# Attention, two mixture layers, one core: GpSimd's elementwise work moved to ScalarE and VectorE

## The chip, the cores and the metric

The kernel runs on one core of a Trainium2 chip. A core has TensorE (matrix products; the profile tells its products, PE, from its weight loads, PEld), VectorE (DVE), ScalarE (ACT), GpSimd (POOL) and SyncE (SP), which issues most DMAs here. Each engine works through its own queue in order and waits on semaphores for the others. The metric is the device time of one execution in microseconds; smaller is better.

## The reference

Three stages follow each other, all float32 (q, k and the last layer's weights are drawn with the spreads the reference sets):

```python
# attention: q, k, v of shape (4, 8, 576, 64), blocks of 64
scores = (q @ k.T) / 8;  scores = where(block_i >= block_j, scores, -1e9)
attn = exp(scores - max) ;  attn = attn / (sum(attn) + 1e-9);  x = attn @ v   # -> (2304, 512)
# first layer: w1, w2, w3 of (512, 768), w_out of (768, 512), held as int64 images of float64 values
h = maximum(maximum(x @ w1, x @ w2), x @ w3);  x = h @ w_out                   # -> (2304, 512)
# last layer: 8 experts of (512, 1024) and (1024, 512)
active = x @ w_skip > 0;  e = argmax(x @ w_gate);  p = softmax(x @ w_gate)[e]
out = x;  out[active] += p * (relu(x @ w1[e]) @ w2[e])
```

## The kernel before

The 2304 tokens are cut into nine chunks of 256. Attention works in 80 *units*: one pair of heads and up to 128 queries (64 in "packed" units, which put both heads into one set of 128 partitions), with 64 to 576 keys. A unit goes through four functions, and three units are under way at a time: unit k in `s_scores`, k-1 in `s_norm` and `s_trans`, k-2 in `s_pv`.

- `s_scores`: TensorE forms `sc` from `q` and `k` (L231) and adds the mask by a small product (L238). VectorE reduces to the negated maximum `nm` (L244, L249, L252, with L247 or L253 where there are two parts), ScalarE takes the exponential with `nm` as bias and sums it (L258). `q` has been multiplied by 0.125 ahead by GpSimd in `prep` (L209). Where the keys don't fill 128 columns, GpSimd clears 64 more (L260).
- `s_norm`: `r` is the sum plus 1e-9 (L270 on VectorE, L273 on GpSimd for chunks 0 to 2, else on VectorE), its reciprocal is taken (L274), and `p` is multiplied by it: on GpSimd for chunks 0 to 3 (L278), on VectorE for the others (L280).
- `s_trans`: TensorE transposes `p` (L293), ScalarE or VectorE copies it out of PSUM (L295, L297).
- `s_pv`: the product with `v` (L312); ScalarE writes the result's high part (L314), VectorE the low part `x` (L315).

The first layer's products run on pairs of a high part (rounded to the product's format) and a low part (what is left), three products for one. `wprep` makes the weights' pairs, 24 tiles of 128x512: a DMA on SP's queue into one of three raw buffers (L148, or L155 for `w_out`), then `decode`: the absolute value on ScalarE (L137), four VectorE operations (L138 to L141), the second half of which reads the raw buffer. ScalarE then writes the high part (L158) and GpSimd the low part `lo` (L159). Tiles 18 to 23 (`w_out`) also go through TensorE to make the routing weights `wp`.

`m_h` does the first layer for one chunk and one of six slices of the hidden width: three groups of twelve products (L327) into one of two PSUM buffers, ScalarE copies the first (`ha`, L331), VectorE takes the maximum (`hm`, L334), ScalarE writes the high part `h_h` (L338), GpSimd the low part `h_l` (L339). `m_logits` (L348) reads `h_h` and `h_l` for the routing, `m_y` (L364) multiplies by `w_out`. Routing (`r_gate`, `r_rank`) and the last layer (`Moe2`, with its own splits into high and low parts on all three engines, L633 and L637) follow.

The program is written as a loop over units; a credit hands out steps of the first layer between them, and `wprep` is called four times per unit until tile 18. The order that each engine gets in the end is made by a planner, which sorts the instructions by its own estimates of when each is ready and gives attention a higher priority than weights and first layer. The last steps of the first layer and the last layer keep the order in which they are written. The `x` tiles have two buffers, so attention for chunk c+2 can't write `x` before chunk c's `m_h` has read it.

Of the kernel before, what the change touches and what calls it, by code (L numbers as in the profile page):

```python
# [12 lines left out]
AF = mybir.ActivationFunctionType  # L13
ALU = mybir.AluOpType
# [7 lines left out]
P = 128  # L22
# [3 lines left out]
ND = DM // P  # L26
# [64 lines left out]
def _moe1_phase(tc, nc, const, small, g):  # L91
# [10 lines left out]
    with ExitStack() as st_y:  # L102
# [25 lines left out]
        raw_t = [apool.tile([P, 4 * P, 2], I32, name=f"raw{i}") for i in range(3)]  # L128
# [13 lines left out]
            return uf  # L142

        def wprep(k):
            raw, dec = raw_t[k % 3], dec_t[k % 6]
            if k < 18:
                f, i = divmod(k, 3)
                nc.sync.dma_start(  # L148
                    out=raw.rearrange("p (c f) t -> p c (f t)", c=ND),
                    in_=ws[i][:, 2 * f * P:2 * (f + 1) * P].rearrange("(c p) f -> p c f", p=P))  # L150
                c = decode(raw, dec).rearrange("p (c f) -> p c f", c=ND)
                hi, lo = w_piece(f, i, 0), w_piece(f, i, 1)
            else:
                f = k - 18
                nc.sync.dma_start(out=raw.rearrange("p f t -> p (f t)"), in_=w_out[f * P:(f + 1) * P, :])  # L155
                c = decode(raw, dec)
                hi, lo = wo[0][:, f, :], wo[1][:, f, :]
            nc.scalar.copy(hi, c)  # L158
            (nc.vector if (0 and k % 0 == 0) else nc.gpsimd).tensor_tensor(lo, c, hi, op=ALU.subtract)  # L159
            if k >= 18:  # L160
                ps = ps_m.tile([P, ND, P], F32, tag="mo", name="pswt")
                for d in range(ND):
                    nc.tensor.transpose(ps[:, d, :], c[:, d * P:(d + 1) * P], ident)
                wt = tmp.tile([P, ND, P], F32, tag="y", name="wt")
                nc.scalar.copy(wt, ps)
                ps = ps_m.tile([P, NG], F32, tag="mo", name="psw")
                for d in range(ND):
                    nc.tensor.matmul(ps, wt[:, d, :], wr_sb[:, d, :], start=(d == 0), stop=(d == ND - 1))
                nc.vector.tensor_copy(wp[:, f, 0:NG], ps)
                nc.vector.tensor_tensor(wp[:, f, NG:2 * NG], ps, wp[:, f, 0:NG], op=ALU.subtract)  # L170
# [24 lines left out]
        def load_v(i):  # L195
            if i >= len(groups):
# [5 lines left out]
            nc.sync.dma_start(  # L202
                out=gd["v"][:, 0:nkt, :],
                in_=v[b, 0:nkt * P, hp * P:(hp + 1) * P].rearrange("(t p) d -> p t d", p=P))

        def prep(i):
            if i < len(groups):
                q = gdat[i]["q"][:, 0:groups[i][3] - groups[i][2]]
                nc.gpsimd.tensor_scalar(q, q, 0.125, None, op0=ALU.mult)  # L209

        units = []
        for i, (c, b, qlo, qhi, tiles, hp) in enumerate(groups):
# [5 lines left out]
        def s_scores(k):  # L218
            i, c, hp, q0, nq, nk, col, first = units[k]
            gd, u = gdat[i], ud[k]  # L220
            packed = nq == 64
            parts = [(0, nk)] if nk <= 512 else [(0, nk // 2), (nk // 2, nk)]
            sets = 1 if packed else 2
            banks = {}
            for n, (lo, hi) in enumerate(parts):
                if n == 0 or not packed:
                    ps = ps_s.tile([P, 2, 512], F32, tag="sc", name="sc")
                for j in range(2):
                    bank = banks[j, n] = ps[64 * j:64 * j + 64, n] if packed else ps[:, j]
                    rows = slice(64 * j, 64 * j + 64)  # L230
                    nc.tensor.matmul(bank[:, 0:hi - lo], gd["q"][rows, q0:q0 + nq], gd["k"][rows, lo:hi],  # L231
                                     start=True, stop=packed or hi != nk)
                if n == 0:
                    first_ps = ps
                if hi == nk and not packed:
                    for j in range(2):
                        rows = slice(64 * j, 64 * j + 64)
                        nc.tensor.matmul(banks[j, n][:, hi - lo - 64:hi - lo], mask_q[rows], mask_k[rows],  # L238
                                         start=False, stop=True)
            pt = pp.tile([P, 2, 5 * P], F32, tag="p", name="p")  # L240
            nm = sm.tile([P, 2], F32, tag="nm", name="nm")
            w = parts[0][1]
            if packed:
                nc.vector.tensor_reduce(nm[:, 0:len(parts)], first_ps[:, 0:len(parts), 0:w], axis=AX.X, op=ALU.max,  # L244
                                        negate=True)
                if len(parts) == 2:
                    nc.vector.tensor_tensor(nm[:, 0:1], nm[:, 0:1], nm[:, 1:2], op=ALU.min)  # L247
            else:
                nc.vector.tensor_reduce(nm, first_ps[:, :, 0:w], axis=AX.X, op=ALU.max, negate=True)  # L249
                if len(parts) == 2:  # L250
                    nm2 = sm.tile([P, 2], F32, tag="nm2", name="nm2")
                    nc.vector.tensor_reduce(nm2, ps[:, :, 0:w], axis=AX.X, op=ALU.max, negate=True)  # L252
                    nc.vector.tensor_tensor(nm, nm, nm2, op=ALU.min)  # L253
            su = sm.tile([P, 2, 2], F32, tag="su", name="su")
            for j in range(sets):
                for n, (lo, hi) in enumerate(parts):
                    src = first_ps[:, n, 0:hi - lo] if packed else banks[j, n][:, 0:hi - lo]
                    nc.scalar.activation(pt[:, j, lo:hi], src, AF.Exp, bias=nm[:, j:j + 1], accum_out=su[:, n, j:j + 1])  # L258
            if nk % P:
                nc.gpsimd.memset(pt[:, 0:sets, nk:nk + 64], 0.0)  # L260
            u.update(p=pt, su=su, parts=len(parts), sets=sets)

        def s_norm(k):
            i, c, hp, q0, nq, nk, col, first = units[k]
            u = ud[k]
            su, sets = u["su"], u["sets"]
            r = sm.tile([P, 2], F32, tag="r", name="r")
            eng = nc.gpsimd if c < 3 else nc.vector
            if u["parts"] == 2:
                nc.vector.scalar_tensor_tensor(r[:, 0:sets], su[:, 0, 0:sets], 1e-9, su[:, 1, 0:sets],  # L270
                                               op0=ALU.add, op1=ALU.add)
            else:
                eng.tensor_scalar(r[:, 0:sets], su[:, 0, 0:sets], 1e-9, None, op0=ALU.add)  # L273
            nc.vector.reciprocal(r[:, 0:sets], r[:, 0:sets])  # L274
            for j in range(sets):
                pt = u["p"][:, j, 0:nk]
                if c < 4:
                    nc.gpsimd.tensor_tensor(pt, pt, r[:, j:j + 1].to_broadcast([P, nk]), op=ALU.mult)  # L278
                else:
                    nc.vector.tensor_scalar(pt, pt, r[:, j:j + 1], None, op0=ALU.mult)  # L280

# [36 lines left out]
        def m_h(c, f):  # L318
            xh, xl = xt[c]
            h_h, h_l = hid[c // (NCH - 1)]  # L320
            prev = None
            for i in range(3):
                ps = ps_m.tile([P, CH], F32, tag="mo", name="ps_h")
                n = 0
                for d in range(ND):
                    for a, x in ((w_piece(f, i, 0), xh), (w_piece(f, i, 0), xl), (w_piece(f, i, 1), xh)):
                        nc.tensor.matmul(ps, a[:, d, :], x[:, d, :], start=(n == 0), stop=(n == 3 * ND - 1))  # L327
                        n += 1
                if i == 0:
                    prev = tmp.tile([P, CH], F32, tag="hm", name="ha", bufs=4)  # L330
                    nc.scalar.copy(prev, ps)  # L331
                else:
                    nxt = tmp.tile([P, CH], F32, tag="hm", name=f"hm{i}", bufs=4)
                    nc.vector.tensor_tensor(nxt, ps, prev, op=ALU.max)  # L334
                    prev = nxt
                if i < 2:
                    yield
            nc.scalar.copy(h_h[:, f, :], prev)  # L338
            nc.gpsimd.tensor_tensor(h_l[:, f, :], prev, h_h[:, f, :], op=ALU.subtract)  # L339
            yield  # L340

        def m_logits(c, rd):
# [120 lines left out]
            nc.vector.memset(mask_q[r:r + 1, 0:64], 1.0)  # L463
            nc.vector.memset(mask_k[r:r + 1], -float(2 ** 30))
        load(0)
        prep(0)
        nc.sync.dma_start(out=g["cst_sb"], in_=g["cst"])
        load_v(0)
        load(1)
# [33 lines left out]
        for k in range(n_u + 2):  # L503
            if k < n_u:
                i, c, first = units[k][0], units[k][1], units[k][-1]
                if first:
                    load(i + 2)
                    load_v(i + 1)
                with pri(c):
                    s_scores(k)  # L510
                if first:
                    prep(i + 1)
            if 0 <= k - 1 < n_u:
                with pri(units[k - 1][1]):
                    s_norm(k - 1)
# [318 lines left out]
```

## Time and profile before

| | us |
|---|---|
| median of 3 runs (lowest, highest) | 749.91 (748.97, 750.33) |
| profiled execution: its time | 748.17 |
| profiled execution: its span, first to last instruction | 746.4 |
| busy: TensorE products / weight loads | 660.3 (88%) / 539.7 |
| busy: VectorE / ScalarE / GpSimd | 405.6 (54%) / 298.2 (40%) / 315.2 (42%) |

The profile is of one execution, 1.7 us below the median of the timed runs; its own time is 1.8 us above its span. Busy shares are means over the whole span, and stages differ much, so the rows below come from views of single stretches. In a view that groups instructions, a line gives the code line, engine and operation, output and inputs, tile, count, then busy time in us and the mean of one in ns, then idle time ahead of them and what ended it.

### The profile page before, as it was taken

Reading aid. Unit: us, or ns where it says so; the run is one execution under the profiler, and the core shown is the slowest. Engines: PE = TensorE matmul, PEld = TensorE weight load, DVE = VectorE, ACT = ScalarE, POOL = GpSimd, SP = SyncE. Lnnn points to the kernel's source line nnn. Section 1 sums busy time; section 2 is a strip of 40 time slices with the busy share of each in tenths; the row PEclk is TensorE's granted clock in tenths of the full one; section 3 lists DMA queues with packets and bytes.
Section 4 is the critical chain, followed back from the end, with each engine's and each line's share of the span. In section 5 each row is a group of like instructions: output and inputs, shape, how many; then the busy total and the mean of one; then the engine's idle time right before and its main releaser. Section 6 shows DMA issues by size and latency. Waiting matters only on the chain. (4 is left out here: it accounts for less than half of the span.)

```text
span 746.4 us, 13347 instructions
## 1 busy us (share of the span) xinstructions
PE 660.3 (88%) x4854; PEld 539.7 (72%) x4854; DVE 405.6 (54%) x915; ACT 298.2 (40%) x751; POOL 315.2 (42%) x346
## 2 busy tenths in 40 slices
PE   5764789999999999999999999999988938786786
PEld 3432578868978987978888887888978726565665
DVE  4999994344246436346434646534237127477763
ACT  4555554443143325234233434424243125163552
POOL 5986884435231202102113222111039239285775
PEclk9997999999999999999999999999999978898989
DMA  6765433221022212011102112002337659566731
GB/s 178 200 196 170 153 111 84 72 77 38 19 78 70 74 58 78 17 45 55 35 31 71 53 49 65 19 18 76 113 113 252 237 152 339 196 187 218 249 130 31
DMA packets 74520, 82.26 MB, mean 110 GB/s; under 512 B 11284, under 2 KB 51348, under 8 KB 74432
## 3 DMA queue, kind: packets, MB, share of 16 engines
q1 hardware_dynamic: 70768, 75.69, 32.4%
q0 software_dynamic: 2624, 5.45, 2.4%
q8 instruction: 48, 0.79, 0.4%
q14 instruction: 40, 0.33, 0.1%
q10 hardware_dynamic: 1040, 0.01, 0.1%
HBM read 70.44 MB, written 11.96 MB: 110 GB/s over the span
## 5 line engine op out<-in xcount | busy, mean ns | idle before, releaser
L327 PE MATMUL ps_h<-x,w 128*128 128x256 f32 x1944 | 269.1, 291 | 12.0 <-DVE hm L334 6.5
L327 PEld LDWEIGHTS ps_h<-x,w 128*128 128x128 f32 x1944 | 243.6, 193 | 33.7 <-issue 13.9
L258 ACT ACTIVATE p<-sc,nm 128x288 f32<-128x288 f32 (+8 forms) x168 | 84.6, 513 | 39.0 <-PE tp L293 20.2
L209 POOL TENSOR_SCALAR q<-q 128x256 f32<-128x256 f32 (+3 forms) x48 | 37.2, 775 | 127.5 <-DMA q<-in_kqT_dram 107.9
L637 POOL TENSOR_TENSOR lo<-raw,hi 128x1024 fp32r<-128x1024 f32 x30 | 83.0, 2788 | 16.4 <-ACTq L765 15.2
L231 PE MATMUL sc<-k,q 64*128 64x288 f32 (+9 forms) x384 | 78.8, 491 | 10.1 <-POOL q L209 8.8
L293 PE MATMUL tp<-cst_sb,p 128*128 128x128 f32 x432 | 76.6, 295 | 12.0 <-DVE x L315 6.9
L339 POOL TENSOR_TENSOR h_l<-hm,h_h 128x256 fp32r<-128x256 f32 x54 | 42.7, 791 | 98.7 <-ACT h_h L338 98.6
L637 DVE TENSOR_TENSOR lo<-raw,hi 128x1024 fp32r<-128x1024 f32 x30 | 73.5, 2457 | 8.7 <-ACT hi L633 6.4
L312 PE MATMUL pv<-pT,vt 128*64 128x128 f32 (+1 forms) x960 | 68.4, 280 | 7.8 <-ACT pT L295 4.2
L293 PEld LDWEIGHTS tp<-cst_sb,p 128*128 128x128 f32 x432 | 52.1, 148 | 25.5 <-issue 11.3
L295 ACT COPY pT<-tp 128x512 f32<-128x512 f32 (+2 forms) x78 | 40.2, 517 | 70.8 <-PE tp L293 69.8
L633 ACT CAST hi<-raw 128x2048 fp32r<-128x2048 f32 x30 | 56.4, 1902 | 29.1 <-PEq L765 18.5
L312 PEld LDWEIGHTS pv<-pT,vt 128*64 128x64 f32 x960 | 49.8, 141 | 22.8 <-ACT pT L295 6.2
L249 DVE TENSOR_REDUCE nm<-sc 128x2 f32<-128x256 f32 (+7 forms) x64 | 51.6, 810 | 22.0 <-PE sc L238 20.9
L297 DVE COPY pT<-tp 128x512 f32<-128x512 f32 (+2 forms) x58 | 32.0, 551 | 52.3 <-PE tp L293 51.9
L278 POOL TENSOR_TENSOR p<-p,r 128x128 f32<-128x128 f32 (+8 forms) x64 | 52.1, 832 | 19.6 <-DVE r L274 13.0
L334 DVE TENSOR_TENSOR hm<-ps_h,ha 128x256 f32<-128x256 f32 x54 | 22.8, 422 | 54.4 <-PE ps_h L327 48.9
L231 PEld LDWEIGHTS sc<-k,q 64*128 64x128 f32 (+1 forms) x384 | 31.4, 190 | 28.8 <-POOL q L209 10.0
L338 ACT CAST h_h<-hm 128x256 fp32r<-128x256 f32 x54 | 22.0, 407 | 74.1 <-DVE hm L334 73.9
L260 POOL MEMSET p<- 128x128 f32 (+1 forms) x48 | 9.1, 189 | 91.2 <-PE tp L293 83.0
L364 PE MATMUL ps_y<-wo_h,h_h 128*128 128x512 f32 x108 | 43.7, 405 | 0.0
(132 smaller groups left out, 944.0 us busy)
## 6 DMA issues: line engine op xcount, KB each, us to landing
raw<-in_m_w_dram SPq DMA_DIRECT2D x32, 1024.0 KB
raw<-in_w_dram SPq DMA_DIRECT2D x18, 512.0 KB
vt<-in_v_dram SPq DMA_DIRECT2D x16, 320.0 KB
x<-y SPq DMA_DIRECT2D x18, 256.0 KB
out_dram<-y SPq DMA_DIRECT2D x18, 256.0 KB
raw<-in_w_out_dram SPq DMA_DIRECT2D x6, 512.0 KB
vt<-in_v_dram SPq DMA_DIRECT2D x8, 256.0 KB
k<-in_kqT_dram SPq DMA_DIRECT2D x32, 64.0 KB
```

Source lines behind the costliest of these rows:

```text
L231: nc.tensor.matmul(bank[:, 0:hi - lo], gd["q"][rows, q0:q0 + nq], gd["k"][rows, lo:hi], start=True, stop=packed or hi != nk)
L249: nc.vector.tensor_reduce(nm, first_ps[:, :, 0:w], axis=AX.X, op=ALU.max, negate=True)
L258: nc.scalar.activation(pt[:, j, lo:hi], src, AF.Exp, bias=nm[:, j:j + 1], accum_out=su[:, n, j:j + 1])
L278: nc.gpsimd.tensor_tensor(pt, pt, r[:, j:j + 1].to_broadcast([P, nk]), op=ALU.mult)
L293: nc.tensor.transpose(tp[:, n, :], u["p"][:, j, t * P:(t + 1) * P], ident)
L295: nc.scalar.copy(pT[:, t0:t0 + len(part)], tp[:, 0:len(part)])
L312: nc.tensor.matmul(pv[64 * j:64 * j + 64, 0:nq], vt[:, t, 64 * j:64 * j + 64], pT, start=(t == 0), stop=(t == nkt - 1))
L327: nc.tensor.matmul(ps, a[:, d, :], x[:, d, :], start=(n == 0), stop=(n == 3 * ND - 1))
L339: nc.gpsimd.tensor_tensor(h_l[:, f, :], prev, h_h[:, f, :], op=ALU.subtract)
L364: nc.tensor.matmul(ps, a[:, f, hs], x[:, f, :], start=(n == 0), stop=(n == 3 * NF - 1))
L633: self.nc.scalar.copy(self.w(e, s)[0], self.raw_of(4 * e + s))
L637: eng.tensor_tensor(lo[:, r], self.raw_of(4 * e + s)[:, r], hi[:, r], op=ALU.subtract)
```

## The change

`q` is no longer scaled: `prep` is gone, and 0.125 enters the exponential as its scale; the maximum is scaled by VectorE instead. In `s_norm` the `r` addition is always on VectorE; the multiplication of `p` is on ScalarE for chunks 0 to 2 (a copy with a scale per partition), on VectorE from chunk 3 on. The low parts of the weights and of `h` are made on VectorE. In `wprep` the low part of a `w_out` tile now stands behind the transposes. GpSimd keeps the clearing of `p`, constants and DMAs there, and its share of the last layer.

```diff
--- before.py
+++ after.py
@@ -142,25 +142,27 @@
             return uf
 
         def wprep(k):
-            raw, dec = raw_t[k % 3], dec_t[k % 6]
+            raw = raw_t[k % len(raw_t)]
             if k < 18:
                 f, i = divmod(k, 3)
                 nc.sync.dma_start(
                     out=raw.rearrange("p (c f) t -> p c (f t)", c=ND),
                     in_=ws[i][:, 2 * f * P:2 * (f + 1) * P].rearrange("(c p) f -> p c f", p=P))
-                c = decode(raw, dec).rearrange("p (c f) -> p c f", c=ND)
                 hi, lo = w_piece(f, i, 0), w_piece(f, i, 1)
             else:
                 f = k - 18
                 nc.sync.dma_start(out=raw.rearrange("p f t -> p (f t)"), in_=w_out[f * P:(f + 1) * P, :])
-                c = decode(raw, dec)
                 hi, lo = wo[0][:, f, :], wo[1][:, f, :]
+            c = decode(raw, dec_t[k % 6])
+            if k < 18:
+                c = c.rearrange("p (c f) -> p c f", c=ND)
             nc.scalar.copy(hi, c)
-            (nc.vector if (0 and k % 0 == 0) else nc.gpsimd).tensor_tensor(lo, c, hi, op=ALU.subtract)
             if k >= 18:
                 ps = ps_m.tile([P, ND, P], F32, tag="mo", name="pswt")
                 for d in range(ND):
                     nc.tensor.transpose(ps[:, d, :], c[:, d * P:(d + 1) * P], ident)
+            nc.vector.tensor_tensor(lo, c, hi, op=ALU.subtract)
+            if k >= 18:
                 wt = tmp.tile([P, ND, P], F32, tag="y", name="wt")
                 nc.scalar.copy(wt, ps)
                 ps = ps_m.tile([P, NG], F32, tag="mo", name="psw")
@@ -202,11 +204,6 @@
             nc.sync.dma_start(
                 out=gd["v"][:, 0:nkt, :],
                 in_=v[b, 0:nkt * P, hp * P:(hp + 1) * P].rearrange("(t p) d -> p t d", p=P))
-
-        def prep(i):
-            if i < len(groups):
-                q = gdat[i]["q"][:, 0:groups[i][3] - groups[i][2]]
-                nc.gpsimd.tensor_scalar(q, q, 0.125, None, op0=ALU.mult)
 
         units = []
         for i, (c, b, qlo, qhi, tiles, hp) in enumerate(groups):
@@ -251,11 +248,13 @@
                     nm2 = sm.tile([P, 2], F32, tag="nm2", name="nm2")
                     nc.vector.tensor_reduce(nm2, ps[:, :, 0:w], axis=AX.X, op=ALU.max, negate=True)
                     nc.vector.tensor_tensor(nm, nm, nm2, op=ALU.min)
+            nc.vector.tensor_scalar(nm[:, 0:sets], nm[:, 0:sets], 0.125, None, op0=ALU.mult)
             su = sm.tile([P, 2, 2], F32, tag="su", name="su")
             for j in range(sets):
                 for n, (lo, hi) in enumerate(parts):
                     src = first_ps[:, n, 0:hi - lo] if packed else banks[j, n][:, 0:hi - lo]
-                    nc.scalar.activation(pt[:, j, lo:hi], src, AF.Exp, bias=nm[:, j:j + 1], accum_out=su[:, n, j:j + 1])
+                    nc.scalar.activation(pt[:, j, lo:hi], src, AF.Exp, bias=nm[:, j:j + 1], scale=0.125,
+                                         accum_out=su[:, n, j:j + 1])
             if nk % P:
                 nc.gpsimd.memset(pt[:, 0:sets, nk:nk + 64], 0.0)
             u.update(p=pt, su=su, parts=len(parts), sets=sets)
@@ -265,17 +264,16 @@
             u = ud[k]
             su, sets = u["su"], u["sets"]
             r = sm.tile([P, 2], F32, tag="r", name="r")
-            eng = nc.gpsimd if c < 3 else nc.vector
             if u["parts"] == 2:
                 nc.vector.scalar_tensor_tensor(r[:, 0:sets], su[:, 0, 0:sets], 1e-9, su[:, 1, 0:sets],
                                                op0=ALU.add, op1=ALU.add)
             else:
-                eng.tensor_scalar(r[:, 0:sets], su[:, 0, 0:sets], 1e-9, None, op0=ALU.add)
+                nc.vector.tensor_scalar(r[:, 0:sets], su[:, 0, 0:sets], 1e-9, None, op0=ALU.add)
             nc.vector.reciprocal(r[:, 0:sets], r[:, 0:sets])
             for j in range(sets):
                 pt = u["p"][:, j, 0:nk]
-                if c < 4:
-                    nc.gpsimd.tensor_tensor(pt, pt, r[:, j:j + 1].to_broadcast([P, nk]), op=ALU.mult)
+                if c < 3:
+                    nc.scalar.activation(pt, pt, AF.Copy, scale=r[:, j:j + 1])
                 else:
                     nc.vector.tensor_scalar(pt, pt, r[:, j:j + 1], None, op0=ALU.mult)
 
@@ -336,7 +334,7 @@
                 if i < 2:
                     yield
             nc.scalar.copy(h_h[:, f, :], prev)
-            nc.gpsimd.tensor_tensor(h_l[:, f, :], prev, h_h[:, f, :], op=ALU.subtract)
+            nc.vector.tensor_tensor(h_l[:, f, :], prev, h_h[:, f, :], op=ALU.subtract)
             yield
 
         def m_logits(c, rd):
@@ -463,7 +461,6 @@
             nc.vector.memset(mask_q[r:r + 1, 0:64], 1.0)
             nc.vector.memset(mask_k[r:r + 1], -float(2 ** 30))
         load(0)
-        prep(0)
         nc.sync.dma_start(out=g["cst_sb"], in_=g["cst"])
         load_v(0)
         load(1)
@@ -508,8 +505,6 @@
                     load_v(i + 1)
                 with pri(c):
                     s_scores(k)
-                if first:
-                    prep(i + 1)
             if 0 <= k - 1 < n_u:
                 with pri(units[k - 1][1]):
                     s_norm(k - 1)
```

## Rows read from the trace of the kernel before

**Rows 1.** Busy by stage: stretch, length; each engine; granted clock, DMA share, GB/s.

```profile
14.50:112.00 97.50, 67.83 (x404) 46.49 (x403) 95.27 (x148) 55.59 (x143) 79.06 (x76) 0.89 0.58 169
...
130.00:540.00 410.00, 409.56 (x3436) 343.90 (x3431) 189.48 (x608) 148.36 (x484) 94.06 (x166) 1.00 0.18 54
540.00:602.00 62.00, 55.62 (x390) 50.07 (x389) 24.74 (x59) 19.99 (x30) 29.95 (x21) 1.00 0.59 203
602.00:746.40 144.40, 102.22 (x422) 79.78 (x421) 84.86 (x63) 60.61 (x53) 95.60 (x49) 0.86 0.58 188
```

**Rows 2.** TensorE's waits, 130 to 540 us: total us, times, longest.

```profile
PE pv L312 <- DVE pT L297: 0.4, 1, 0.4
```

**Rows 3.** TensorE's waits, 0 to 130 us.

```profile
PE sc L231 <- POOL q L209: 8.8, 3, 6.1
PE tp L293 <- DVE x L315: 6.9, 3, 4.3
```

**Rows 4.** Waits of SP's queue, 0 to 130 us.

```profile
SPq L148 <- DVE dec L141: 16.4, 12, 2.7
```

**Rows 5.** VectorE grouped by line and shape, 14.5 to 112 us.

```profile
L141 DVE SCALAR_TENSOR_TENSOR dec<-raw,dec 128x512 int32<-128x512 int32 x24 | 23.8, 992 | 0.1
L140 DVE SCALAR_TENSOR_TENSOR dec<-raw,dec 128x512 int32<-128x512 int32 x24 | 23.4, 976 | 0.2
L139 DVE TENSOR_SCALAR dec<-dec 128x512 int32<-128x512 int32 x24 | 18.4, 767 | 0.1
L138 DVE TENSOR_SCALAR dec<-dec 128x512 f32<-128x512 f32 x24 | 16.9, 704 | 1.0 <-ACT dec L137 1.0
...
L274 DVE RECIPROCAL r<-r 128x2 f32<-128x2 f32 x13 | 2.0, 158 | 0.4
L334 DVE TENSOR_TENSOR hm<-ps_h,ha 128x256 f32<-128x256 f32 x4 | 1.7, 414 | 1.2 <-PE ps_h L327 1.2
```

**Rows 6.** VectorE in order of time, 46 to 50 us: start, duration, instruction.

```profile
46.27 0.41 DVE L138 TENSOR_SCALAR dec<-dec 128x512 f32<-128x512 f32 x1
46.60 0.68 DVE L140 SCALAR_TENSOR_TENSOR dec<-raw,dec 128x512 int32<-128x512 int32 x1
47.21 0.41 DVE L139 TENSOR_SCALAR dec<-dec 128x512 int32<-128x512 int32 x1
47.54 0.68 DVE L141 SCALAR_TENSOR_TENSOR dec<-raw,dec 128x512 int32<-128x512 int32 x1
...
48.22 1.68 DVE L140 SCALAR_TENSOR_TENSOR dec<-raw,dec 128x512 int32<-128x512 int32 x1
```

**Rows 7.** GpSimd in order of time, 45 to 50 us.

```profile
47.74 1.61 POOL L159 TENSOR_TENSOR w<-dec,w 128x512 fp32r<-128x512 f32 x1
```

**Rows 8.** Single lines over the whole span: count, shortest/median/longest in ns, first and last start.

```profile
L140 DVE SCALAR_TENSOR_TENSOR dec<-raw,dec x24: 673/693/1698, 15.8 to 109.8; 128x512 int32<-128x512 int32 x24
...
L637 DVE TENSOR_TENSOR lo<-raw,hi x30: 1211/1226/8665, 556.4 to 732.0; 128x1024 fp32r<-128x1024 f32 x30
...
L273 DVE TENSOR_SCALAR r<-su x40: 146/169/343, 159.3 to 505.7; 128x2 f32<-128x2 f32 x36, 128x1 f32<-128x1 f32 x4
...
L339 POOL TENSOR_TENSOR h_l<-hm,h_h x54: 722/736/1723, 86.8 to 583.0; 128x256 fp32r<-128x256 f32 x54
```

**Rows 9.** ScalarE grouped by line and shape, 14.5 to 112 us.

```profile
L258 ACT ACTIVATE p<-sc,nm 128x512 f32<-128x512 f32 x8 | 5.5, 692 | 0.0
L258 ACT ACTIVATE p<-sc,nm 128x384 f32<-128x384 f32 x8 | 4.6, 591 | 0.0
...
L258 ACT ACTIVATE p<-sc,nm 128x256 f32<-128x256 f32 x6 | 2.8, 472 | 1.2 <-DVE nm L249 1.2
...
L258 ACT ACTIVATE p<-sc,nm 128x128 f32<-128x128 f32 x4 | 1.5, 381 | 0.0
```

**Rows 10.** GpSimd grouped by line and shape, 0 to 130 us.

```profile
L278 POOL TENSOR_TENSOR p<-p,r 128x512 f32<-128x512 f32 x8 | 10.4, 1320 | 0.3 <-DVE r L274 0.3
```

**Rows 11.** Waits, 530 to 612 us.

```profile
PE ps_l L348 <- POOL h_l L339: 1.1, 2, 0.6
```

## The prediction

> **What bounds the kernel now.** I read the table by stage first [rows 1]. From 130 to 540 us TensorE is busy for 409.56 of 410 us at full granted clock, and the list of its waits for that stretch holds 0.4 us in all [rows 2]. VectorE has 189.48 us of work there, ScalarE 148.36, GpSimd 94.06. So in this long stage TensorE is the bound, and work that moves between the other three changes nothing as long as none of them gets late. From 602 us on runs the last layer, which the change does not touch.
>
> The ramp, 14.5 to 112 us, is the other way round: VectorE is busy for 95.27 of 97.5 us, TensorE only for 67.83, ScalarE for 55.59 [rows 1]. In it the 24 weight tiles are decoded while the first attention units run. TensorE's largest waits up to 130 us are for GpSimd's scaled `q` (8.8 us) and for VectorE's `x` (6.9 us) [rows 3]. SP's queue waits for VectorE too: the next raw weights may only be loaded once a decode has freed their buffer (16.4 us in 12 waits for `w1` to `w3`) [rows 4]. So VectorE sets the length of the ramp, and each us that the ramp loses should come off the end, since TensorE does the same work behind it without a gap.
>
> Why is VectorE full there? Four decode operations a tile make up most of it, with means of 704, 767, 976 and 992 ns [rows 5]. The order in time shows that these are not their own durations: one of each of the four, at 46.27 to 48.2 us, took 0.41, 0.68, 0.41 and 0.68 us, and right after it the same L140 took 1.68 us [rows 6], while GpSimd's `lo` subtraction started at 47.74 and ran for 1.61 us [rows 7]. The shortest L140 is 673 ns, the longest 1698 [rows 8]. VectorE and GpSimd hold each other up, and the change takes GpSimd's elementwise work away.
>
> **The change part by part.**
>
> *Decode without GpSimd.* A tile costs 0.704+0.767+0.976+0.992 = 3.44 us on average [rows 5] against 0.41+0.68+0.41+0.68 = 2.18 us undisturbed [rows 6]. 24 x 1.26 = 30.2 us less on VectorE. From below: nothing, if VectorE's long operations had another cause than GpSimd; from above 30.2, since 2.18 is about the minimum.
>
> *Low parts on VectorE.* 24 new subtractions of 128x512 with two SBUF inputs. The nearest rows are L140, which has the same shape and occupies 0.61 us from its start to the next start (46.60 to 47.21) [rows 6], and the 128x1024 `lo` on VectorE in the last layer, whose minimum and median are 1211 and 1226 ns, half of which is 0.61 [rows 8]. 24 x 0.61 = 14.6 us; at L140's full 0.68 it would be 16.3.
>
> *Small operations.* Each unit gains a multiplication of `nm` by 0.125 and, in chunks 0 to 2, the `r` addition from GpSimd; the ramp holds 14 units (13 reciprocals of two columns [rows 5] and one of one). Each new operation depends on its predecessor; an `r` addition on VectorE takes 0.17 us [rows 8]. 14 x 2 x 0.17 = 4.8 us. Four `h_l` in the ramp at 0.41 us, as the four `hm` of the same shape [rows 5], are 1.7 us.
>
> VectorE's ramp thus loses 30.2 - 14.6 - 4.8 - 1.7 = 9.1 us.
>
> *Scaling on ScalarE.* Two instructions a unit (one in packed units). No row has a copy from SBUF with a scale per partition; the bounds are nothing and the exponential of the same width: 0.692, 0.591, 0.472 and 0.381 us at 512, 384, 256 and 128 columns [rows 9]. With eight of each for chunks 0 and 1 that is at most 17.1 us, and ScalarE would have 55.6 + 17.1 = 72.7 of some 88 us. I take the upper end, and count it at nothing in the sum, because VectorE stays the fuller engine. On the path of one unit it even gains: GpSimd took 1.32 us for 512 columns [rows 10]. The cover is gone if decode's own ScalarE steps (absolute value and the high part's cast) then wait behind it.
>
> The Trainium skill has a rule that speaks against this part: "ScalarE: Activation LUTs", section "Rules for kernel authors", says that multiplications belong on VectorE, not on ScalarE; by its section "What ACT_TABLE_LOAD costs" I estimate 280 + 0.833 x 512 = 707 ns for the wide copy. No run here shows that copy; the exponential of that width, 692 ns, lies close. By that rule alone scaling is best put on VectorE, which would lengthen the full engine; the table by stage decides for ScalarE here.
>
> *`q` no longer scaled.* 0.125 goes into the exponential's scale, which L258 applies without an instruction of its own; the product `q`-`k` then starts when the DMA has landed. TensorE's 8.8 us of waiting for it lie inside the VectorE-bound ramp, so I count nothing, with 8.8 us as the other end.
>
> *Steady stage.* VectorE gets about 43 `h_l` (18 us), 66 `nm` (11 us) and the scaling of chunk 3, on top of 189.5 of 410 us [rows 1]: some 55 to 60%. TensorE hides it: nothing, with the fourth case below as the other end.
>
> *End of the first layer (540 to 602 us).* TensorE waits 1.1 us in two places for the last `h_l` [rows 11]; at `hm`'s 0.41 us on VectorE [rows 5] instead of GpSimd's median of 0.74 [rows 8] that is 2 x 0.33 = 0.7 us less. Bounds: -1.1 and, if `h_l` queues behind one of VectorE's `lo` of 1.2 us, +1.2.
>
> *What is late next.* VectorE stood idle for 97.5 - 95.27 = 2.2 us of the ramp [rows 1]. With shorter operations the loads of raw weights and ScalarE's steps come closer to it, and the planner orders every engine anew, for which no row gives a price; I give back the same again, 2.2 us.
>
> **The sum:** -9.1 - 0.7 + 2.2 = -7.6 us. The profiled execution took 748.17 us, which gives 740.6; the median of the runs shown is 1.74 us above that execution, which would give 742.3. I forecast 741.5.
>
> **The rivals.**
>
> *More than VectorE's saving.* The chain of one unit also gets shorter: no wait for `q`, scaling in half the time. Then TensorE, which stood idle for 97.5 - 67.8 = 29.7 us in the ramp, gets its attention work earlier, and the 8.8 us [rows 3] go as well: 740.6 - 8.8 = 731.8 us. For it: the scaling stands between exponential and transposes of each unit, and TensorE works in order. Against: VectorE has no gap that a shorter chain could fill.
>
> *ScalarE takes VectorE's place.* Its queue is in order, and each of the 24 decodes begins and ends with a ScalarE step. If scaling delays the two together by 0.32 us, 24 x 0.32 = 7.6 us are given back: 748.2 us, no change. For it: 72.7 of 88 us, above the 0.57 share of now. Against: still idle for a sixth. The skill's rule above points this way.
>
> *VectorE blocked in the stage that TensorE bounds (slower).* `h_l` can only run when ScalarE has written `h_h`. GpSimd could stand and wait; VectorE, in order, has the next `hm`, `nm` and `x` queued behind it, and for `hm` TensorE waits with two PSUM buffers. If each of the 43 `h_l` of this stage holds TensorE for one step of `hm`'s length, 0.41 us, that is +17.6 us, and 740.6 + 17.6 = 758.2. It decides from 7.6/17.6 = 43% of them on. Against: TensorE waits for 0.4 us of 410 now, and VectorE's queue is half empty.
>
> *The change does not do what it says*, VectorE's long operations staying long: then the 21.1 us of additions stand alone in the ramp. [rows 6] and [rows 7] leave little room; I count it with the slower case.
>
> **How the numbers follow.** Forecast 0.46, more gain 0.22, ScalarE 0.18, slower 0.14. The range of 729 to 750 us takes in the first three with 2 to 3 us of scatter and leaves out the last. A measurement of this kernel tells 0.2%, or 1.5 us, from no change. Faster: the first two and a part of the third with half of its loss, 0.74; within it 0.13; slower 0.13.
>
> **What would show it.** Right: L138 to L141 near 0.41, 0.41, 0.68 and 0.68 us on average; VectorE's full stretch ends about 10 us earlier than at 112 us; from 130 us on TensorE still has no waits; the first `ps_l` still comes without one. Wrong: long gaps on VectorE before decode steps that wait for ScalarE (third case); new TensorE waits for `hm` between 130 and 540 us (fourth); a TensorE that is full well before 100 us (second).

## The result and the profile after

The changed kernel takes 728.29 us (median of 4, 726.87 to 732.82) against 749.44 us in the same runs (748.48 to 750.33): a ratio of 0.9728, with a 95% interval of 0.9684 to 0.9773. The forecast was 741.5 us. The time lies just below the range of 729 to 750 us, and near the 731.8 us of the first rival, "More than VectorE's saving". Where the highest time of a kernel below lies far above its median, that execution ran at a lower granted clock than the kernel's others, so medians are what to compare.

The profiled execution of after took 727.8 us with a span of 726.0, 20.4 us less than the span before. This is the table by stage after (stretch, length, busy time of TensorE, its weight loads, VectorE, ScalarE and GpSimd, granted clock, DMA share, GB/s). Up to 540 us the stretches are those of [rows 1].

```profile
14.50:112.00 97.50, 86.91 (x628) 64.22 (x622) 87.15 (x231) 79.27 (x204) 0.76 (x5) 0.93 0.66 189
...
130.00:540.00 410.00, 405.76 (x3350) 342.99 (x3349) 213.01 (x707) 148.36 (x460) 28.45 (x54) 1.00 0.19 58
```

In the ramp TensorE went from 67.83 to 86.91 us, and ran 628 instructions instead of 404. VectorE went from 95.27 to 87.15 us with 231 instructions instead of 148, ScalarE from 55.59 to 79.27, GpSimd from 79.06 to 0.76.

A fixed point in the program shows how much of the ramp is gone: the first product for the router's logits, `ps_l`, of the first chunk. Here are its instructions before and then after (count, shortest/median/longest ns, first and last start).

```profile
L348 PE MATMUL ps_l<-h_h,wp x54: 274/276/362, 147.5 to 583.0; 128*20 128x256 f32 x54
```

```profile
L346 PE MATMUL ps_l<-h_h,wp x54: 276/277/362, 125.8 to 562.4; 128*20 128x256 f32 x54
```

It starts 21.7 us earlier, and the last one starts 20.6 us earlier: little is gained or lost in between. The stretch from the span's start to that point, before and after:

```profile
0.00:147.50 147.50, 109.99 (x808) 80.28 (x809) 113.21 (x215) 77.99 (x216) 103.59 (x132) 0.93 0.51 146
```

```profile
0.00:125.80 125.80, 109.26 (x813) 80.65 (x814) 100.87 (x295) 95.69 (x260) 3.44 (x20) 0.93 0.60 172
```

TensorE does the same work at the same mean clock in both, 110.0 and 109.3 us. So its idle time there fell from 147.5 - 110.0 = 37.5 us to 125.8 - 109.3 = 16.5 us. Those 21.0 us are, within a microsecond, the whole gain.

TensorE's waits up to 130 us after, beside [rows 3] (total us, times, longest):

```profile
PE sc L228 <- ACT p L256: 6.1, 6, 2.4
PE sc L228 <- DMA q<-in_kq_dram: 3.8, 1, 3.8
PE ps_h L325 <- ACT w L159: 2.3, 1, 2.3
PE tp L291 <- ACT pT L293: 1.6, 2, 1.3
PE tp L291 <- DVE x L313: 0.8, 1, 0.8
```

The 8.8 us for GpSimd's `q` have become 3.8 us for the DMA that brings it, and the 6.9 us for `x` are 0.8. The largest entry is now ScalarE's exponential. Before, the list went on below the two lines of [rows 3]:

```profile
PE ps_h L327 <- DVE hm L334: 5.1, 2, 3.3
PE tp L293 <- ACT pT L295: 4.9, 3, 3.0
PE pv L312 <- ACT pT L295: 4.2, 1, 4.2
PE pv L312 <- DVE x L315: 3.0, 2, 1.7
...
PE sc L231 <- ACT p L258: 1.3, 3, 0.7
```

The whole lists hold 37.1 us before (up to 147.5 us) and 16.1 after, so they account for TensorE's idle time. What went is 9.1 us of waits for VectorE's `x`, 7.0 for ScalarE's copies `pT`, 5.1 for `hm`, 5.0 for `q` and 2.9 in smaller ones. What came is 4.8 us for the exponential and 3.3 in smaller ones. So the wait for `q` is a quarter of the gain; most of it lies behind VectorE and ScalarE steps of the units' chains. A wait is put down to the step that came last, not to what had delayed that step.

VectorE by line up to 130 us, after (busy us, mean ns, idle before):

```profile
L140 DVE SCALAR_TENSOR_TENSOR dec<-raw,dec 128x512 int32<-128x512 int32 x24 | 16.4, 684 | 0.0
L141 DVE SCALAR_TENSOR_TENSOR dec<-raw,dec 128x512 int32<-128x512 int32 x24 | 16.4, 683 | 0.0
...
L164 DVE TENSOR_TENSOR w<-dec,w 128x512 fp32r<-128x512 f32 x18 | 12.3, 684 | 0.1
L138 DVE TENSOR_SCALAR dec<-dec 128x512 f32<-128x512 f32 x24 | 10.1, 423 | 4.9 <-ACT dec L137 4.8
L139 DVE TENSOR_SCALAR dec<-dec 128x512 int32<-128x512 int32 x24 | 10.0, 417 | 0.0
...
L251 DVE TENSOR_SCALAR nm<-nm 128x2 f32<-128x2 f32 (+1 forms) x28 | 4.5, 159 | 0.2
```

The four steps take 0.42, 0.42, 0.68 and 0.68 us, where [rows 5] have 0.70, 0.77, 0.98 and 0.99. But the decode does not end earlier. L141, its last step, has its first and last start here:

```profile
L141 DVE SCALAR_TENSOR_TENSOR dec<-raw,dec x24: 679/683/689, 19.1 to 114.2; 128x512 int32<-128x512 int32 x24
```

Before, the last one started at 110.5 us. VectorE ran 231 instructions in the ramp instead of 148: the time that it won went into the steps of attention, which the order now puts between those of the decode.

Scaling on ScalarE, by shape, up to 130 us after:

```profile
L256 ACT ACTIVATE p<-sc,nm 128x512 f32<-128x512 f32 x8 | 5.5, 700 | 0.0
L276 ACT ACTIVATE p<-p,r 128x512 f32<-128x512 f32 x8 | 5.4, 733 | 0.0
```

The scaled copy (L276) costs 33 ns more than the exponential of the same width.

At the end of the first layer, TensorE's waits from 505 to 575 us after:

```profile
PE ps_h L325 <- DVE hm L332: 3.4, 3, 1.7
PE ps_h L325 <- ACT ha L329: 1.7, 3, 0.8
...
PE ps_l L346 <- DVE h_l L337: 0.2, 1, 0.2
```

The wait for `h_l` has gone from the 1.1 us of [rows 11] to 0.2, while that for `hm` has grown (before it was 1.3 us in 530 to 612 us). From the eighth chunk's first `ps_l` to `tg`, the routing result that the last layer's gathers read, it took 50.1 us before and 52.5 after. For 130 to 510 us the list of TensorE's waits is empty.

### The profile page after: what moved, and what is told of

It is laid out like the page before. It is cut to its first block, busy times and chain, and to the rows that moved or that the text cites. A ratio compares the mean times of both kernels' runs of the same rounds, so it can differ in the third digit from the quotient of the medians.

```text
span 726.0 us, 13283 instructions
## 1 busy us (share of the span) xinstructions
PE 659.5 (91%) x4854; PEld 539.4 (74%) x4854; DVE 421.2 (58%) x1113; ACT 316.7 (44%) x799; POOL 139.8 (19%) x132
## 5 line engine op out<-in xcount | busy, mean ns | idle before, releaser
L228 PE MATMUL sc<-k,q 64*128 64x288 f32 (+9 forms) x384 | 77.3, 480 | 10.0 <-ACT p L256 6.1
L632 POOL TENSOR_TENSOR lo<-raw,hi 128x1024 fp32r<-128x1024 f32 x30 | 81.2, 2731 | 22.1 <-ACTq L760 15.2
L632 DVE TENSOR_TENSOR lo<-raw,hi 128x1024 fp32r<-128x1024 f32 x30 | 75.6, 2527 | 8.1 <-ACT hi L628 5.9
L295 DVE COPY pT<-tp 128x512 f32<-128x512 f32 (+2 forms) x58 | 32.0, 551 | 42.7 <-PE tp L291 41.1
L416 POOL DMA_INDIRECT table<-pair,sloti x18 | 17.6, 980 | 149.8 <-DVE sloti L413 134.2
L312 ACT CAST x<-pv 128x128 fp32r<-128x128 f32 (+1 forms) x80 | 19.9, 257 | 56.9 <-PE pv L310 38.6
L362 PE MATMUL ps_y<-wo_h,h_l 128*128 128x512 f32 x108 | 42.6, 395 | 0.0
```

Of the source, the lines that this page charges most:

```text
L295: nc.vector.tensor_copy(pT[:, t0:t0 + len(part)], tp[:, 0:len(part)])
L362: nc.tensor.matmul(ps, a[:, f, hs], x[:, f, :], start=(n == 0), stop=(n == 3 * NF - 1))
L632: eng.tensor_tensor(lo[:, r], self.raw_of(4 * e + s)[:, r], hi[:, r], op=ALU.subtract)
```

## The experiments

Theory A, which the parts below test: the two engines' hold-up is the cause, and with it gone each unit's chain is shorter and TensorE starves less. Rival B: the gain comes from the shorter chains alone, `q` and the scaling, and GpSimd's load does not matter. The expectations, which were put on record before their runs, call them theory 1 and theory 2; there e2, e3 and e4 are the runs with the low parts, the scaling or `q` taken back, and e5 is the first filler. Each run's ratio is to the kernel before, run on the same chip.

**The hold-up put back, the order kept.** The changed kernel with 60 unused GpSimd multiplications from one scratch row to another, which nothing waits for; the order of the instructions on TensorE, VectorE and ScalarE is that of after.

```diff
+        scr = apool.tile([P, 2, 576], F32, name="scr")
...
+                nc.gpsimd.memset(scr, 0.0)
+                for _ in range(60):
+                    nc.gpsimd.tensor_tensor(scr[:, 1, 0:512], scr[:, 0, 0:512], scr[:, 0, 0:512], op=ALU.mult)
```

> The changed kernel, and GpSimd runs 60 multiplications of 128x512 from scratch to scratch from about 3 us on (some 80 us of work) that wait for nobody and that nobody waits for; the order of instructions on TensorE, VectorE and ScalarE is the changed kernel's to the last one. Theory 1 (mutual hold-up of VectorE and GpSimd): L140, L141 and the low parts rise from 0.68 to 0.95 us or more, 745 to 765 us, nearly all that the change brought is gone. Theory 2 (GpSimd's slow steps on a unit's path): nothing is on a path, 727 to 730 us.

755.16 us (10 runs, 749.98 to 761.67), ratio 1.0069 [1.0041, 1.0097]: the whole gain is gone and a little more. GpSimd's filler in this kernel, and VectorE by line up to 130 us (lines lie one further down than in after):

```profile
L526 POOL TENSOR_TENSOR scr<-scr 128x512 f32<-128x512 f32 x60 | 71.8, 1196 | 4.5
```

```profile
L142 DVE SCALAR_TENSOR_TENSOR dec<-raw,dec 128x512 int32<-128x512 int32 x21 | 20.3, 964 | 0.0
L141 DVE SCALAR_TENSOR_TENSOR dec<-raw,dec 128x512 int32<-128x512 int32 x21 | 19.3, 919 | 0.0
L165 DVE TENSOR_TENSOR w<-dec,w 128x512 fp32r<-128x512 f32 x18 | 16.7, 928 | 0.0
L140 DVE TENSOR_SCALAR dec<-dec 128x512 int32<-128x512 int32 x22 | 14.1, 643 | 0.0
...
L139 DVE TENSOR_SCALAR dec<-dec 128x512 f32<-128x512 f32 x22 | 12.9, 589 | 0.8 <-ACT dec L138 0.8
...
L272 DVE TENSOR_SCALAR r<-su 128x2 f32<-128x2 f32 x16 | 8.1, 506 | 5.6 <-ACT p L257 5.6
...
L273 DVE RECIPROCAL r<-r 128x2 f32<-128x2 f32 (+1 forms) x20 | 3.1, 155 | 0.0
```

Work that no instruction waits for lengthens L141, the 684 ns step of after, to 919 ns; the filler ends at 69 us, so the means up to 130 us mix steps beside it and steps behind it. The filler keeps no other GpSimd work waiting either: in after GpSimd has nothing to do from 2.3 to 79.5 us, and the waits of TensorE, VectorE and ScalarE up to the first `ps_l` here name no GpSimd step. That `ps_l` starts at 153.8 us. Up to there:

```profile
0.00:153.80 153.80, 115.75 (x812) 82.59 (x813) 134.06 (x295) 97.61 (x260) 76.46 (x81) 0.88 0.49 140
```

TensorE stands idle for 153.8 - 115.75 = 38.0 us, as before the change. The other 6.5 us of the 28.0 that it is late are the same work at a mean granted clock of 0.88 instead of 0.93. Rival B is out: with the shorter chains, but with GpSimd busy, nothing is left. Nor is the planner's new order enough by itself, since this kernel has it.

**A filler that only writes.** The same place and order, with a fill instead of a multiplication.

```diff
...
+                for _ in range(60):
+                    nc.gpsimd.memset(scr, 0.0)
```

> As the last, but GpSimd's 60 operations only write (clearing 128x1152, about as long each), and read nothing. The order on the other engines is the changed kernel's again. If any GpSimd work holds VectorE up, as e5. The Trainium skill (SBUF — State Buffer, Who interferes with whom) says that a VectorE instruction with two SBUF inputs contends only with a GpSimd one that reads; then L140, L141 and the low parts stay at 0.68 us, at most the one-input L138 and L139 grow, and the time is 730 to 738 us.

738.07 us (736.57, 737.87, 738.28 and 748.58), ratio 0.9893 [0.981, 0.9976]; the medians alone give 0.9845. About 10 us of the gain are gone, where the filler that reads took 27. VectorE by line up to 130 us:

```profile
L139 DVE TENSOR_SCALAR dec<-dec 128x512 f32<-128x512 f32 x24 | 17.5, 727 | 1.5 <-ACT dec L138 1.5
L141 DVE SCALAR_TENSOR_TENSOR dec<-raw,dec 128x512 int32<-128x512 int32 x24 | 16.5, 689 | 0.0
L142 DVE SCALAR_TENSOR_TENSOR dec<-raw,dec 128x512 int32<-128x512 int32 x24 | 16.3, 681 | 0.0
L140 DVE TENSOR_SCALAR dec<-dec 128x512 int32<-128x512 int32 x24 | 16.3, 679 | 0.0
...
L252 DVE TENSOR_SCALAR nm<-nm 128x2 f32<-128x2 f32 (+1 forms) x24 | 12.4, 518 | 0.1
```

Steps with two inputs (L141, L142) keep their 0.68 us, steps with one (L139, L140) go from 0.42 to 0.73 and 0.68. The Trainium skill ("SBUF — State Buffer", section "Who interferes with whom") says that a VectorE instruction with two SBUF inputs contends with a GpSimd instruction that reads SBUF and not with one that only writes, while `tensor_scalar` can contend with GpSimd in its two-port modes. The two fillers agree for the steps with two inputs: 0.68 us beside writes, 0.92 and 0.96 beside reads. The steps with one input are held up by writes as well; which mode they ran in no trace here shows.

**The two GpSimd jobs repeated into scratch.** The subtraction of the low parts and the scaling stay where the change put them, and GpSimd does each once more for nothing.

```diff
...
+            nc.gpsimd.tensor_tensor(scr[1][:, 0:512] ..., c, hi, op=ALU.subtract)
...
+                    nc.gpsimd.tensor_tensor(scr[1][:, 0:nk], scr[0][:, 0:nk], r[:, j:j + 1].to_broadcast([P, nk]), op=ALU.mult)
```

> The changed kernel, and GpSimd besides repeats the low parts of the 24 weight tiles and a multiplication by r for the units of chunks 0 to 3 into a scratch tile that nobody reads: GpSimd is as busy in the ramp as before, but no other engine waits for its results. If mutual hold-up of VectorE and GpSimd makes the ramp long (theory 1): decode operations L139 to L141 above 0.7 us on average again and 740 us or more. If the time came from GpSimd's slow steps on the path of each attention unit (theory 2): 727 to 731 us, whatever VectorE's means do.

769.03 us, ratio 1.0252 [1.0202, 1.0302]. The decode steps with two inputs take 0.94 and 0.85 us, those with one 0.48 and 0.52. But here the repeats read what attention and the decode make, the planner ordered the engines anew, and attention's steps came later. From 14.5 to 112 us:

```profile
14.50:112.00 97.50, 51.53 (x275) 34.48 (x276) 92.68 (x166) 56.55 (x137) 49.20 (x42) 0.68 0.54 156
```

TensorE got 275 instructions done and ran at a mean granted clock of 0.68. Between the levels of 0.5 (1.2 GHz) and 1, that is some 64% of the stretch at the lower one. Hold-up, new order and low clock can't be parted here; the run with the order kept was made for that.

**One part taken back.** From the changed kernel, each part alone goes back to GpSimd. The low parts of the weights:

```diff
-            nc.vector.tensor_tensor(lo, c, hi, op=ALU.subtract)
+            nc.gpsimd.tensor_tensor(lo, c, hi, op=ALU.subtract)
```

> The changed kernel with the weights' low parts back on GpSimd. VectorE loses 24 x 0.68 us of own work and gets 35 us of GpSimd work beside its decode. Theory 1: decode steps grow by some 0.3 us each, 24 x 4 x 0.3 - 16 = +13 us on VectorE, 735 to 741 us. Theory 2: low parts are not on a unit's path, 725 to 729 us.

The scaling of chunks 0 to 3:

```diff
-                if c < 3:
-                    nc.scalar.activation(pt, pt, AF.Copy, scale=r[:, j:j + 1])
+                if c < 4:
+                    nc.gpsimd.tensor_tensor(pt, pt, r[:, j:j + 1].to_broadcast([P, nk]), op=ALU.mult)
```

> The changed kernel with the multiplication of p by r back on GpSimd for chunks 0 to 3. Theory 2: it stands between exponential and transposes of each unit, 2 x 0.7 us longer for each of 16 units: 736 to 745 us. Theory 1: about 28 us of GpSimd work in the ramp beside VectorE, 732 to 738 us, with longer decode steps.

The scaling of `q`, with the factor gone from exponential and `nm`:

```diff
...
+                nc.gpsimd.tensor_scalar(q, q, 0.125, None, op0=ALU.mult)
...
```

> The changed kernel with q scaled by GpSimd ahead of the products again and no factor in the exponential. Theory 2: TensorE waits for q again in the first units, up to 8.8 us: 731 to 737 us. Theory 1: 12 short GpSimd operations in the ramp, 728 to 730 us.

**One part alone.** The kernel before with only that part of the change: the scaling on ScalarE (chunk 3 on VectorE), the weights' low parts on VectorE, or 0.125 in the exponential.

> The kernel before with one part of the change: p is multiplied by r on ScalarE in chunks 0 to 2 and on VectorE in chunk 3; q, the low parts, h_l and the r addition stay on GpSimd. If the parts add up, it brings what taking it back cost (e3): 749 - 15 = 734 us. If the parts need each other (one GpSimd part left is enough to hold VectorE up): 742 us or more.

> The kernel before with the weights' low parts on VectorE alone. If the parts add up: 749 - 7 = 742 us, as e2. By my sum for VectorE, with GpSimd's other work still beside it: about a third of 30 us less, 16 us more, so +6, 755 us.

> The kernel before with 0.125 in the exponential and no scaling of q on GpSimd. If the parts add up: 749 - 2.6 = 746 us, as e4. If TensorE's 8.8 us of waiting for q are all lost time: 740 us.

The six together, with the kernel itself (TensorE's idle time is the start of the first `ps_l` less TensorE's busy time until then; before has 147.5, 37.5 and 113.2):

| kernel | median us | ratio, 95% | first `ps_l` | TensorE idle until then | VectorE busy until then |
|---|---|---|---|---|---|
| after | 728.29 | 0.9728 [0.9684, 0.9773] | 125.8 | 16.5 | 100.9 |
| after, low parts back | 735.5 | 0.9827 [0.9779, 0.9876] | 128.9 | 19.7 | 104.6 |
| after, scaling back | 743.92 | 0.9911 [0.9875, 0.9947] | 135.7 | 27.4 | 112.1 |
| after, `q` back | 730.89 | 0.974 [0.9682, 0.9798] | 127.2 | 22.1 | 100.2 |
| before, scaling alone | 738.34 | 0.9863 [0.982, 0.9906] | 139.2 | 34.8 | 103.0 |
| before, low parts alone | 742.1 | 0.9907 [0.9868, 0.9946] | 140.1 | 32.1 | 112.6 |
| before, 0.125 alone | 742.2 | 0.9926 [0.99, 0.9953] | 142.3 | 33.3 | 116.4 |

Alone, the parts bring 1.37%, 0.93% and 0.74%, which adds up to 3.0%, and the whole brings 2.72% (each with an interval of 0.3 to 0.5% to either side). So they add up within what can be measured; `h_l` and the `r` addition were not run alone. The scaling is the largest, both alone (where its interval overlaps that of the low parts) and taken back. Scaling alone, at 738.34 us, lies between its two expected times.

The four decode steps of a tile take 3.44 us before and 2.21 after. With the low parts back they take 2.65, with the scaling back 2.47, with `q` back 2.22, with one part alone 2.64 to 3.27: the low parts and the scaling each bring back a piece of the hold-up, `q` hardly any. The times don't follow that alone, for the kernel with the scaling back has the shorter decode steps and is 8 us slower than the one with the low parts back. The latter fits the range of theory 1, the former that of theory 2, so hold-up and chain both count. With one part alone the first `ps_l` comes 5.2 to 8.3 us earlier, but only 2.7 to 5.4 us of that are TensorE's idle time; its busy time for the same work differs as well.

With `q` alone VectorE is as full as before, and the kernel gains all the same; TensorE's waits up to 130 us in that kernel:

```profile
PE sc L231 <- ACT p L259: 5.7, 5, 2.6
...
PE sc L231 <- DMA q<-in_kq_dram: 3.8, 1, 3.8
```

The 8.8 us for `q` are 3.8 for its DMA, as in after. In the kernel with `q` back a wait of 8.0 us for GpSimd's `q` returns, yet the time differs from after by less than the interval and lies between the two theories. The planner orders each of these kernels anew, and the stage between the eighth and the ninth chunk's first `ps_l` then takes from 34.0 (before) and 36.5 (after) to 43.7 us (scaling back), so a part taken back doesn't have one clean price.

**The scaling on VectorE instead of ScalarE.** Without GpSimd work, so without hold-up.

```diff
-                if c < 3:
-                    nc.scalar.activation(pt, pt, AF.Copy, scale=r[:, j:j + 1])
-                else:
-                    nc.vector.tensor_scalar(pt, pt, r[:, j:j + 1], None, op0=ALU.mult)
+                nc.vector.tensor_scalar(pt, pt, r[:, j:j + 1], None, op0=ALU.mult)
```

> The changed kernel with the multiplication of p by r on VectorE in chunks 0 to 2 too, so GpSimd stays out. If VectorE's total sets the ramp's length: 14 to 18 units with two operations of 0.25 to 0.42 us are +8 to +12 us, 736 to 740 us. If only hold-up counted: ScalarE loses 18 us, 726 to 729 us.

744.88 us (10 runs), ratio 0.9936 [0.9904, 0.9968]; 16.6 us of the gain are gone, more than either expectation had. From the start to the first `ps_l`, then TensorE's largest wait up to 130 us:

```profile
0.00:137.90 137.90, 111.44 (x808) 82.87 (x809) 112.80 (x340) 78.15 (x216) 3.43 (x19) 0.84 0.53 156
```

```profile
PE sc L228 <- ACT p L256: 11.2, 9, 1.9
```

VectorE's decode steps keep 0.42 and 0.69 us, and still TensorE is idle for 137.9 - 111.4 = 26.5 us, 10 us more than in after. Another 2 us until the first `ps_l` are the same work at a mean granted clock of 0.84 instead of 0.93, and 6.2 us come at the end of the first layer, where the stage named above took 42.7 us; the last layer then took some 3 us less. VectorE's work up to the first `ps_l`, 112.8 us, is that of the kernel before (113.2), and yet that `ps_l` comes 9.6 us earlier than there. From this kernel to after VectorE's work falls by another 11.9 us and the start by 12.1. So which engine takes the scaling counts besides the freeing of GpSimd.

**Two versions that go on.** In the last layer each pair of 128x1024 `lo` is split between VectorE and GpSimd. Those lines read SBUF on both engines at once; after, from 575 to 727 us on VectorE:

```profile
L632 DVE TENSOR_TENSOR lo<-raw,hi 128x1024 fp32r<-128x1024 f32 x24 | 60.1, 2513 | 8.1 <-ACT hi L628 5.9 <-issue 1.9 <-DVEq L760 0.3
```

The median of the line over the whole span is 1.23 us and its longest 8.65, so most of these instructions run free and some wait long. What TensorE waits for most there, besides the gather:

```profile
PE psy L664 <- DVE Two_l L651: 12.1, 3, 5.8
PE psb L664 <- DVE Two_l L651: 4.6, 1, 4.6
```

The version gives all the `lo` to VectorE, in four places:

```diff
-        self.split_lo(e, s, 1, self.nc.gpsimd)
+        self.split_lo(e, s, 1, self.nc.vector)
```

> The changed kernel with the last layer's low parts all on VectorE as well (GpSimd keeps its indirect DMAs). If the hold-up is the same there, two halves of 1.22 us one after the other take VectorE no longer than one half beside GpSimd does now (2.5 us on average), and the waits of TensorE for Two_l (12.1 and 4.6 us) shrink: 715 to 724 us. If VectorE is then too full: 728 to 735 us.

715.06 us (714.06 to 718.78), ratio 0.9556 [0.9509, 0.9603]: the best of all, about 13 us below the changed kernel. Its rows for VectorE from 560 to 713 us, and TensorE's waits there:

```profile
L632 DVE TENSOR_TENSOR lo<-raw,hi 128x1024 fp32r<-128x1024 f32 x48 | 56.0, 1220 | 3.9 <-ACT hi L628 2.6 <-DVEq L760 1.3
```

```profile
PE psa L648 <- DMA xgs<-x,tg: 12.6, 1, 12.6
PE psa L664 <- DVE lo L632: 10.0, 4, 2.5
```

Twice the instructions take VectorE less time: 48 x 1.22 = 58.6 us against 24 x 2.51 = 60.3. TensorE's waits for `Two_l` fall from 18.2 to 3.7 us in all, and those for `lo` rise from 3.1 to 10.0. From `tg` (577.3 and 576.6 us) to the end the last layer went from 148.7 to 135.7 us; in the twelve kernels that leave it alone it takes 145.4 to 149.6.

With a fourth buffer for the raw weights on top, so that the decode waits less for loads:

```diff
-        raw_t = [apool.tile([P, 4 * P, 2], I32, name=f"raw{i}") for i in range(3)]
+        raw_t = [apool.tile([P, 4 * P, 2], I32, name=f"raw{i}") for i in range(4)]
```

> The kernel of v1 with four raw weight buffers for three. ScalarE waits 13.9 us for raw weights up to 130 us in v1; if that holds the ramp, 3 to 8 us less than v1, 707 to 712 us; if TensorE is fed by attention meanwhile, 713 to 716 us.

721.0 us, ratio 0.964 [0.9589, 0.969], no gain over the version without it. The decode ended at 104.8 us, some 10 us earlier than in after, and the first `ps_l` came at 129.9, 3 us later than in the version without the buffer. That is outside both expected ranges. The planner ordered the engines anew here too, but an earlier end of the decode did not bring the first layer forward.

## Why the prediction was wrong in size

**What was right.** *Decode without GpSimd*: 24 x (3.44 - 2.21) = 29.6 us against the 30.2 predicted, and the filler shows that GpSimd is the cause. *Low parts on VectorE*: 24 x 0.684 = 16.4 us of busy time, the upper of the two values weighed (14.6 was taken). *Small operations*: 0.16 us each, against 0.17 assumed. *Steady stage*: no wait of TensorE from 130 to 510 us. The case *VectorE blocked in the stage that TensorE bounds* did not come: `h_l` makes VectorE wait 15.0 us for `h_h` over the whole span, and TensorE waits 0.2 us of that:

```profile
L337 DVE TENSOR_TENSOR h_l<-hm,h_h x54: 402/426/1730, 63.1 to 562.4; 128x256 fp32r<-128x256 f32 x54
...
  ACT h_h L336: 15.0, 27
```

**The step that failed** is the one under "What bounds the kernel now": "So VectorE sets the length of the ramp". What the sentence goes on to say held: the 21.7 us by which the first `ps_l` came earlier were 20.4 us at the end. From the failed half followed a gain equal to VectorE's net saving, 9.1 us, and nothing for *Scaling on ScalarE* and for *`q` no longer scaled*. Measured, VectorE's busy time until the first `ps_l` fell by 12.3 us (113.2 to 100.9), and TensorE's idle time until then by 21.0. VectorE's sum alone does not set the length: with the scaling on VectorE or back on GpSimd it has as much to do until then as before (112.8 and 112.1 us), and the first `ps_l` comes 9.6 and 11.8 us earlier. VectorE was full, but it was full of two things: a decode whose end TensorE doesn't wait for at once, and the short steps of attention on which each unit's chain hangs. The waits that went are for steps of those chains (`x`, `pT`, `hm`, `q`); that they were late because they stood behind decode steps of up to 1.7 us and behind GpSimd's 1.3 us scaling is argued from the order, not shown step by step. The last decode step started 3.7 us later than before, and the span was still 20.4 us shorter.

The terms that were set at nothing measure, alone, 11 us for the scaling (738.34 against 749.32 in those runs) and 7.1 us for `q` (742.2). Part of the scaling's share is that GpSimd's reads go (the decode steps fall from 3.44 to 3.05 us a tile), so it is not ScalarE's speed alone. That it matters too which engine takes the work, the kernel with scaling on VectorE shows (16.6 us).

**The rivals.** *More than VectorE's saving* named the mechanism and gave 731.8 us, and its sign came: from 50 to 90 us TensorE is busy for 39.2 of 40 us, 25.8 before. That its number is near is partly luck, for it added only the 8.8 us for `q`, of which 3.8 stay, and nothing for the waits for `x`, `pT` and `hm`. Its objection, "VectorE has no gap that a shorter chain could fill", was wrong, as 0.125 alone shows: VectorE is busy for 95.52 of the 97.5 us there, and the first `ps_l` comes 5.2 us earlier. *ScalarE takes VectorE's place* did not come about, though ScalarE is busy for 79 of 97.5 us, about the share (72.7 of 88) that was worked out. TensorE's waits for the exponential rose from 1.3 to 6.1 us, but they can't be put down to the scaling there: they are 5.7 us with 0.125 alone and 11.2 with the scaling on VectorE. The Trainium skill's rule weighed there ("ScalarE: Activation LUTs", section "Rules for kernel authors", multiplications on VectorE) would have lost 16.6 us here. The estimate of 707 ns made from that page for the wide copy stands beside 733 measured.

**Small terms.** *End of the first layer*: -0.7 predicted, +2.4 measured in the two profiled executions, past the upper bound of +1.2: TensorE waits less for `h_l`, but 2.1 us more for `hm`. *What is late next* was set at +2.2 and can't be told apart from the planner's new order.

**What stays open**: how the 21 us divide between hold-up, shorter chains and order. Only the two fillers kept the order; they show that with VectorE held up nothing of the gain is left, not how much each chain brings with it. And the kernels with the scaling on VectorE or GpSimd, or with `q` back, lose 5 to 7 us in a stage far behind the ramp, for which no run was made.

## What to carry to other kernels

Where a busy engine feeds both long background work and short steps of a chain, count a gain by when a fixed point of the program comes and by the waits of the engine that starves until then, not by the net work of the fullest engine. Before counting a move between VectorE and GpSimd, compare an instruction's mean with its shortest duration; a gap there is a price that the busy share hides, and two halves on one engine can then be quicker than one on each. An unused filler on one engine, with the order kept, tells whether the hold-up costs time or only busy share.

## What was not expected of the hardware

Small instructions are held up too: those of 128x2 lose as much in the mean as large ones, 0.16 us becoming 0.52 (`nm` with the filling GpSimd, L252) and 0.51 (`r` with the multiplying one, L272), while the reciprocal of the same shape keeps its 0.155 us with the multiplying one (L273). A part of these means can be time behind a held-up instruction just ahead, since the records of successive instructions overlap. A scaled copy on ScalarE (733 ns at 512 columns) is no cheaper than an exponential (700 ns), the reading out of the exponential's sum left aside.
